# Two-layer state-space kernel, part A: turn tables relative to each 512-step chunk, kept in SBUF, and one wide multiply and one wide add for each turn

## The chip, the cores and the metric

The kernel runs on one core of one Trainium2 chip. The metric is the device time of one execution in microseconds (us), from the first to the last instruction. The core has five engines that work side by side, each through its own list of instructions, strictly in the order of that list: TensorE (PE, matrix products), VectorE (DVE), ScalarE (ACT), GpSimd (POOL) and SyncE (SP, which here only issues transfers). ACT and POOL issue transfers (DMAs) as well.

## The reference

The input is `x` (2048 steps of 640 channels) for part A, and `q`, `k`, `v` of the same shape for part B. The two results stand side by side in the output, 2048 x 1280, bfloat16. Part A is a diagonal complex recurrence over the steps; part B shifts and multiplies `k` and `v`, convolves along the steps by a 4096-point transform and multiplies with `q`.

```python
# part A
dt = exp(log_dt);  Lam_bar = exp(dt * Lam)               # 640 complex states
B_bar = ((Lam_bar - 1.0) / Lam)[:, None] * Bmat
Bu = einsum("bld,pd->blp", x, B_bar)
for t in range(L):  h = Lam_bar * h + Bu[:, t, :]
y = 2.0 * einsum("blp,dp->bld", hseq, Cmat).real + x * Dskip
# part B
kv = (k shifted by 0..3 steps, weighted with shift_k, summed) * v
y = irfft(rfft(kv_pad) * rfft(ssm_k_pad))[:S]
return concat([a, q * (y + kv * ssm_D)], axis=-1)
```

## The kernel before

**Part A.** The 2048 steps are cut into 4 chunks `c` of 512 steps, the 640 states into 5 blocks `j` of 128 (states on partitions, steps along the free axis). `block(c, j)` forms the real and imaginary input with ten matmuls (L352, L355), ACT casts them out of PSUM as `z` (L358, [128, 2, 512] bfloat16), and DVE does the rest. The complex recurrence is made real: the input is turned back by the angle of the state's own rotation at each step (`wre`, `wim`: four multiplies and two adds, L366 to L371), two scans with the real decay `rr` run along the 512 steps (L376, L377), and the result is turned forward again (`hre`, `him`: six instructions, L386 to L391). All of these are 128x512 instructions in bfloat16. The last element of each scan is copied (L381, L382) and starts the scan of the next chunk. After the fifth block of a chunk `project(c)` multiplies the ten `h` tiles with the output matrices: four groups of 20 matmuls (L406, L407) and a few for the skip term (L415), each group cast by ACT as `yo` (L418) and sent out by a transfer that POOL issues.

The angle counts from step 0 of the whole sequence. The sine and cosine of the first 512 steps (`tb_base`) are made once for each `j` by `build_tables` (a multiply on POOL, L316, which writes `tb_ph`; three passes on ACT, L318 to L321) and are written to a table in DRAM (`trig_tab`, L322, issued by POOL). Every block but the first fetches its table again (`tbase`, L337, issued by POOL). In the chunks c = 1, 2, 3 the table is turned by the chunk's start angle: two passes on ACT (`tbA`, `tbB`, L344, L345) and two scalar-tensor-tensor instructions on DVE (`sct`, L347, L348).

**Part B.** The channels are cut into 5 groups `G` of 128. `front(G)` transposes `k` and `v` in (L483, L484, issued by SP), makes `kvT` on DVE (L493, three L495, L497, 2048 wide), and stages it with eight transfers (`kv_st`, L500, SP) and the filter with eight more (`h_st`, L491, SP); a first transform stage on PE is cast by ACT as `As` (L454), a second as `Hf` (L514). `back1(G)` transforms `kv` (`Xs`, L535) and multiplies in frequency on DVE (`pw`, `Y`, 30 instructions). `back2(G)` transforms back on PE, casts four `Zs` (L581), transposes them as `Zt` by a transfer that ACT issues (L583), multiplies with the constant `Mq` (32 matmuls, L593, two halves of 16), and DVE multiplies each half with `q` out of PSUM (`ob`, two L595). POOL issues the transfer out.

Constants for part B are built at the start: `build_G` makes `Gre`, `Gim`, `nGim` in six rounds (an index pattern `t_v` at L102 and a multiply `t_ph` at L104 on POOL, four passes on ACT that end with `Gre`, L112). `build_Mq` makes `Mq`: a small multiply of `m_cv` (128x64, L161) and four multiplies (L164) on POOL, after a cosine on ACT.

**What sets the order.** The source emits blocks of part A at marked points of part B. A scheduler then fixes one list for every engine, from which no engine departs, and tiles that share a name or a tag share a buffer: who writes next waits for the last reader. So a change of a few instructions, or of a tile's tag, can move instructions of other parts of the kernel.

## Time and profile before

| | |
|---|---|
| median of 3 runs | 354.78 us (353.11, 354.78, 356.89) |
| span of the profiled execution | 354.2 us |
| DVE busy | 282.7 us (80%), 619 instructions |
| PE busy | 235.3 us (66%), 1896 matmuls |
| ACT busy | 173.1 us (49%) |
| POOL busy | 85.3 us (24%) |
| mean granted clock of PE | 0.877 of full speed |

The profile records one execution, not one of the three timed ones; the time of that execution is its span, and no other time for it is given. "DVE" and the other names stand for instructions of that engine; "SPq", "ACTq" and "POOLq" are the issuing of transfers by these engines, "issue" in the chain is time in which the engine waited for nothing that the profile shows. In a row of the timeline the first number is the start in us from the beginning of the span, the second the duration; what stands in brackets is the idle time of the engine just ahead of the row and what ended it. In the view of waits the three numbers are the idle time in all, the number of waits, and the longest.

### The profile page before, as it was taken

The page shows a single profiled execution, that of the slowest core. Times are in us where ns is not written, and L with a number is a line of the kernel's source. Part 1 is how long each engine was busy: PE and PEld are TensorE (multiplying, and loading weights), DVE is VectorE, ACT ScalarE, POOL GpSimd, SP SyncE. Part 2 cuts the span into 40 slices and gives each one's busy share as a digit, 9 for nine tenths or more (in the row PEclk, how much of TensorE's full clock was granted, in tenths as well). Part 3 has the DMA queues.
Part 4 walks back from the last instruction along what each step waited for, and adds up shares of the span by engine and source line. Part 5 has one row for each costly group of instructions (what it writes and reads, how often), then busy time and mean ns, then how long its engine had stood idle before and what let it go on. Part 6 is the DMA issues. An engine that isn't in the chain of part 4 may idle for free.

```text
span 354.2 us, 5098 instructions
## 1 busy us (share of the span) xinstructions
PE 235.3 (66%) x1896; PEld 150.7 (43%) x1896; DVE 282.7 (80%) x619; ACT 173.1 (49%) x231; POOL 85.3 (24%) x99
## 2 busy tenths in 40 slices
PE   0058179303799874757898198588499997675591
PEld 0013055301564542544655065265286554464371
DVE  3809999984999999998970799999974896989502
ACT  3548748303357484246564216478254795245020
POOL 2943639993120000020210001001041000020021
PEclk9998859856699999699999789589699999699698
DMA  5999997101035544283757704020664012232312
GB/s 95 197 209 213 205 213 150 44 0 61 19 102 141 112 105 108 71 161 64 179 137 153 170 1 121 20 71 30 148 166 149 1 31 54 66 102 61 76 57 78
DMA packets 89802, 36.68 MB, mean 104 GB/s; under 512 B 76465, under 2 KB 86706, under 8 KB 89778
## 3 DMA queue, kind: packets, MB, share of 16 engines
q1 hardware_dynamic: 65330, 18.01, 25.6%
q0 software_dynamic: 3808, 13.11, 12.5%
q10 hardware_dynamic: 20640, 5.24, 6.5%
q8 instruction: 15, 0.25, 0.3%
q14 instruction: 9, 0.07, 0.1%
HBM read 9.19 MB, written 6.55 MB: 44 GB/s over the span
## 4 chain that ended last, share of the span: by engine, by line
issue 36%; DVE 24%; POOL 12%; PE 9%; SPq 8%; DMA 6%; ACT 3%; ACTq 1%; POOLq 0%; DVEq 0%
POOL m_cv L161 7%; DVE kvT L495 4%; DVE uim L377 2%; PE psB L452 2%; DVE ure L376 2%; SPq L483 2%; DMA Zt<-Zs 2%; DMA out_dram<-yo 2%; PE psB L593 2%; SPq L500 1%; PE psA L406 1%; DMA vT<-in_B_v_dram 1%; PE psA L407 1%; SPq L209 1%; ACTq L583 1%
## 5 line engine op out<-in xcount | busy, mean ns | idle before, releaser
L406 PE MATMUL psA<-Csre,hre 128*128 128x320 bf16 x160 | 49.2, 330 | 40.8 <-DVE hre L388 21.0
L352 PE MATMUL psA<-xT,BTre 128*128 128x512 bf16 x100 | 31.1, 417 | 32.5 <-DMA xT<-in_A_x_dram 20.9
L407 PE MATMUL psA<-Csimn,him 128*128 128x320 bf16 x160 | 49.1, 327 | 1.3 <-DVE him L391 1.2
L337 POOL DMA_DIRECT2D tbase<-trig_tab x15 | 10.8, 721 | 120.4 <-DVE sct L348 75.5
L535 ACT CAST Xs<-psB 128x1024 bf16<-128x1024 f32 (+1 forms) x25 | 21.9, 886 | 36.1 <-PE psB L475 18.5
L358 ACT CAST z<-psA 128x1024 bf16<-128x1024 f32 x20 | 20.1, 1014 | 26.4 <-PE psA L355 15.5
L407 PEld LDWEIGHTS <-him 128*128 128x128 bf16 x160 | 16.7, 105 | 30.2 <-issue 18.7
L406 PEld LDWEIGHTS <-hre 128*128 128x128 bf16 x160 | 16.4, 105 | 30.2 <-DVE hre L388 24.4
L352 PEld LDWEIGHTS <-BTre 128*128 128x128 bf16 x100 | 10.1, 104 | 43.6 <-issue 25.6
L593 PE MATMUL psB<-Mq,Zt 128*128 128x256 bf16 x160 | 24.3, 323 | 6.6 <-DMA Zt<-Zs 6.6
L452 PE MATMUL psB<-R,h_st 128*128 128x512 bf16 x80 | 24.6, 449 | 5.9 <-ACT As_h L454 2.1
L514 ACT CAST Hf<-psB 128x1024 bf16<-128x1024 f32 (+1 forms) x25 | 21.0, 891 | 15.2 <-PE psB L475 10.6
L355 PE MATMUL psA<-xT,BTim 128*128 128x512 bf16 x100 | 27.7, 391 | 0.0
L161 POOL TENSOR_TENSOR m_cv<-m_cv,m_coef 128x64 f32<-128x64 f32 x1 | 25.2, 25237 | 4.1 <-ACT m_cv L50 4.1
L418 ACT CAST yo<-psA 128x640 bf16<-128x640 f32 x16 | 11.0, 694 | 28.6 <-PE psA L415 22.9
L454 ACT CAST As_h<-psB 128x1024 bf16<-128x1024 f32 x20 | 19.9, 1012 | 9.4 <-PE psB L452 9.4
L595 DVE TENSOR_TENSOR ob<-psB,qin 128x1024 bf16<-128x1024 f32 x10 | 12.1, 1217 | 15.0 <-PE psB L593 15.0
L593 PEld LDWEIGHTS <-Zt 128*128 128x128 bf16 x160 | 18.5, 117 | 12.8 <-DMA Zt<-Zs 7.5
L420 POOL DMA_DIRECT2D out_dram<-yo x16 | 8.9, 559 | 55.0 <-ACT yo L418 54.9
L344 ACT ACTIVATE tbA<-tbase,rot_s 128x512 bf16<-128x512 bf16 x15 | 10.9, 725 | 22.7 <-DVE sct L347 19.0
L598 POOL DMA_DIRECT2D out_dram<-ob x5 | 5.9, 1178 | 63.6 <-DVE ob L595 63.6
L581 ACT CAST Zs<-psB 128x1024 bf16<-128x1024 f32 x20 | 19.6, 1011 | 1.4 <-PE psB L580 1.4
(629 smaller groups left out, 780.9 us busy)
## 6 DMA issues: line engine op xcount, KB each, us to landing
tbase<-trig_tab POOLq DMA_DIRECT2D x15, 256.0 KB, 3.3
qin<-in_B_q_dram POOLq DMA_DIRECT2D x5, 512.0 KB, 6.3
h_st<-in_B_ssm_k_dram SPq DMA_DIRECT2D x40, 64.0 KB, 2.1
kv_st<-kvT SPq DMA_DIRECT2D x40, 64.0 KB, 2.4
out_dram<-yo POOLq DMA_DIRECT2D x16, 160.0 KB, 2.1
out_dram<-ob POOLq DMA_DIRECT2D x5, 512.0 KB, 4.6
trig_tab<-tb_base POOLq DMA_DIRECT2D x5, 256.0 KB, 5.0
kT<-in_B_k_dram SPq DMA_TRANSPOSE x5, 6.7
```

Of the source, the lines that this page charges most:

```text
L161: g.tensor_tensor(out=cv[:], in0=cv[:], in1=bq(coef), op=ALU.mult)
L352: nc.tensor.matmul(pz[:, 0, :], lhsT=self.BTre[:, k, j * 128:(j + 1) * 128], rhs=xT[:, k, :], start=(k == 0), stop=(k == NT - 1))
L355: nc.tensor.matmul(pz[:, 1, :], lhsT=self.BTim[:, k, j * 128:(j + 1) * 128], rhs=xT[:, k, :], start=(k == 0), stop=(k == NT - 1))
L358: nc.scalar.copy(out=z[:], in_=pz[:])
L406: nc.tensor.matmul(py[:, b, 0:320], lhsT=Hs[j][0][:, ts], rhs=self.Csre[:, j, c0:c0 + 320], start=(j == 0), stop=False)
L407: nc.tensor.matmul(py[:, b, 0:320], lhsT=Hs[j][1][:, ts], rhs=self.Csimn[:, j, c0:c0 + 320], start=False, stop=False)
L452: nc.tensor.matmul(pa[:, i, :], lhsT=st[:, d8, a_lo * 128:(a_lo + 1) * 128], rhs=self.C.R[:, a_lo, :], start=(a_lo == 0), stop=(a_lo == 1))
L454: nc.scalar.copy(out=As[:, :, 32 * pr:32 * pr + 32].rearrange("p k (i g) -> p k i g", i=2), in_=pa[:].rearrange("p i (g k) -> p k i g", k=32))
L514: nc.scalar.copy(out=Hf[:, :, pos * 128:(pos + n) * 128], in_=pt[:, :, 0:n * 128])
L535: nc.scalar.copy(out=Xs[:, :, 0:W], in_=pt[:, :, 0:W])
L581: nc.scalar.copy(out=Zs[:, qd, :, :].rearrange("p s (c k) -> p s c k", k=8), in_=pzf.rearrange("p (k s c) -> p s c k", k=8, s=8))
L593: nc.tensor.matmul(pyf[:, s4 * 256:(s4 + 1) * 256], lhsT=Zt[:, qd, st_, :], rhs=C.Mq[:, qd, :], start=(qd == 0), stop=(qd == 3))
```

## The change

Two things change in part A, and one line in the building of `Gre`.

The angle now counts from the start of each chunk. One table for each `j` then serves all four chunks, and it stays in SBUF: `tab` [128, 5, 3, 512], whose three slots hold -sin, cos and sin (the first is made by a new multiply by -1 on DVE, line 320 of the new kernel). Slots 0 and 1 and slots 1 and 2, read as two overlapping pairs, give one operand of shape [128, 2, 2, 512]. At the end of a chunk the state is turned by the angle of 512 steps: three instructions on two elements (`cm` twice, `cr`), in the place of the two copies. `trig_tab`, the fetches `tbase`, the ACT passes `tbA` and `tbB` and the two `sct` instructions are gone.

Each turn is now one multiply of 128x2048 (`pr`, line 345; `po`, line 363), whose other operand, `z` or the scan's result `u`, is repeated through a step of zero, and one add of 128x1024 (`w`, line 347; `h`, line 365), in the place of six 128x512 instructions. The scans are as they were.

In `build_G` the index pattern `t_v` now shares the buffer of `t_aph`, the intermediate of the cosine; the next round's pattern then waits for ACT's `Gre` of the round before. The temporaries `cs_tmp` share buffers of `w` and `u`.

```diff
-            v = tp.tile([128, 3, 128], i32, name="t_v")
+            v = tp.tile([128, 3, 128], i32, name="t_v", tag="t_aph")
...
-        self.hpool = ctx.enter_context(tc.tile_pool(name="a_h", bufs=2 * NT + 2))
-        self.dram = ctx.enter_context(tc.tile_pool(name="a_dram", bufs=1, space=bass.MemoryType.DRAM))
-        self.tab = self.dram.tile([NT, 2, 128, CW], bf16, name="trig_tab")
+        self.hpool = ctx.enter_context(tc.tile_pool(name="a_h", bufs=NT + 1))
...
-                tmp = ctp.tile([128, D], bf16, name="cs_tmp")
+                tmp = self.work.tile([128, D], bf16, name="cs_tmp", tag="w")
...
+        self.rot = self.small.tile([128, 2, NT, 2], f32, name="rot")
+        nc.scalar.activation(out=self.rot[:, 1, :, 0], in_=phc[:], func=ACT.Sin, scale=SC)
+        nc.scalar.activation(out=self.rot[:, 1, :, 1], in_=phc[:], func=ACT.Sin, scale=-SC)
...
+        self.tab = self.const.tile([128, NT, 3, CW], bf16, name="tab")
...
     def build_tables(self, j, tp):
-        nc = self.nc
+        nc = self.nc
+        tab = self.tab[:, j, :, :]
         ph = tp.tile([128, CW], i32, name="tb_ph", tag="t_ph")
         nc.gpsimd.tensor_tensor(out=ph[:], in0=self.lo_idx[:], in1=self.Fi[:, j:j + 1].to_broadcast([128, CW]), op=ALU.mult)
-        base = self.tbpool.tile([128, 2, CW], bf16, name="tb_base")
-        nc.scalar.activation(out=base[:, 0, :], in_=ph[:], func=ACT.Sin, scale=SC)
         aph = tp.tile([128, CW], f32, name="tb_aph", tag="t_aph")
         nc.scalar.activation(out=aph[:], in_=ph[:], func=ACT.Abs, scale=SC)
-        nc.scalar.activation(out=base[:, 1, :], in_=aph[:], func=ACT.Sin, bias=self.hpi[:, 0:1], scale=-1.0)
-        nc.gpsimd.dma_start(out=self.tab[j].rearrange("s p t -> p s t"), in_=base[:])
-        return base
+        nc.scalar.activation(out=tab[:, 2, :], in_=ph[:], func=ACT.Sin, scale=SC)
+        nc.scalar.activation(out=tab[:, 1, :], in_=aph[:], func=ACT.Sin, bias=self.hpi[:, 0:1], scale=-1.0)
+        nc.vector.tensor_scalar_mul(out=tab[:, 0, :], in0=tab[:, 2, :], scalar1=-1.0)
...
-            nc.gpsimd.dma_start(out=base[:], in_=self.tab[j].rearrange("s p t -> p s t"))
...
-            nc.scalar.activation(out=tA[:], in_=base[:, 1, :], func=ACT.Copy, scale=sb)
-            nc.scalar.activation(out=tB[:], in_=base[:, 1, :], func=ACT.Copy, scale=cb)
-            sct = work2.tile([128, 2, CW], bf16, name="sct")
-            nc.vector.scalar_tensor_tensor(out=sct[:, 0, :], in0=base[:, 0, :], scalar=cb, in1=tA[:], op0=ALU.mult, op1=ALU.add)
-            nc.vector.scalar_tensor_tensor(out=sct[:, 1, :], in0=base[:, 0, :], scalar=nsb, in1=tB[:], op0=ALU.mult, op1=ALU.add)
...
-        nc.vector.tensor_tensor(out=t1[:], in0=cosT, in1=zre, op=ALU.mult)
-        nc.vector.tensor_tensor(out=t2[:], in0=sinT, in1=zim, op=ALU.mult)
-        nc.vector.tensor_tensor(out=wre[:], in0=t1[:], in1=t2[:], op=ALU.add)
...
+        one = self.tab[:, j, 0, :]
+        tab = bass.AP(one.tensor, one.offset, [one.ap[0], [CW, 2], [CW, 2], [1, CW]])
+        sh = [128, 2, 2, CW]
+
+        pr = work2.tile(sh, bf16, name="pr", tag="pp")
+        nc.vector.tensor_tensor(out=pr[:], in0=tab, in1=z[:].rearrange("p (o b) t -> p o b t", o=1).to_broadcast(sh), op=ALU.mult)
+        w = work.tile([128, 2, CW], bf16, name="w")
+        nc.vector.tensor_tensor(out=w[:], in0=pr[:, :, 0, :], in1=pr[:, :, 1, :], op=ALU.add)
...
+            m = self.small.tile([128, 2, 2], f32, name=f"cm{j}_{c % 2}")
+            last = u[:, :, CW - 1]
+            nc.vector.tensor_tensor(out=m[:, 0, :], in0=last, in1=self.rot[:, 0, j, :], op=ALU.mult)
+            nc.vector.tensor_tensor(out=m[:, 1, :], in0=u[:, ::-1, CW - 1], in1=self.rot[:, 1, j, :], op=ALU.mult)
+            cr = self.small.tile([128, 2], f32, name=f"cr{j}_{c % 2}")
+            nc.vector.tensor_tensor(out=cr[:], in0=m[:, 0, :], in1=m[:, 1, :], op=ALU.add)
+            self.carry[j] = cr
+
+        po = work2.tile(sh, bf16, name="po", tag="pp")
+        nc.vector.tensor_tensor(out=po[:], in0=tab, in1=u[:].rearrange("p a (o t) -> p a o t", o=1).to_broadcast(sh), op=ALU.mult)
+        h = self.hpool.tile([128, 2, CW], bf16, name="h", tag="h")
+        nc.vector.tensor_tensor(out=h[:], in0=po[:, 0, :, :], in1=po[:, 1, :, :], op=ALU.add)
```

The change also moves instructions that it doesn't name, at three places on which the prediction rests.

On POOL, at the start of the program, the list before has the multiply of `m_cv` and the four of `Mq` behind three of the table multiplies `tb_ph` and their transfers:

```order
L316 TENSOR_TENSOR tb_ph<-tb_lo,Fi 128x512 x2
L322 DMA trig_tab<-tb_base 128x2x512
L316 TENSOR_TENSOR tb_ph<-tb_lo,Fi 128x512
L322 DMA trig_tab<-tb_base 128x2x512
L337 DMA tbase<-trig_tab 128x2x512
L161 TENSOR_TENSOR m_cv<-m_cv,m_coef 128x64
L164 TENSOR_TENSOR Mq<-m_cv,m_mask 128x256 x4
L316 TENSOR_TENSOR tb_ph<-tb_lo,Fi 128x512
L322 DMA trig_tab<-tb_base 128x2x512 x2
```

The list after has them inside the rounds of `build_G` (`t_v`, `t_ph`), and the four table multiplies come at the end:

```order
L104 TENSOR_TENSOR t_ph<-t_v,g_bsh 128x384
L161 TENSOR_TENSOR m_cv<-m_cv,m_coef 128x64
L164 TENSOR_TENSOR Mq<-m_cv,m_mask 128x256 x4
L102 IOTA t_v 128x384
L104 TENSOR_TENSOR t_ph<-t_v,g_bsh 128x384
L102 IOTA t_v 128x384
L104 TENSOR_TENSOR t_ph<-t_v,g_bsh 128x384
L102 IOTA t_v 128x384
L104 TENSOR_TENSOR t_ph<-t_v,g_bsh 128x384
L102 IOTA t_v 128x256
L104 TENSOR_TENSOR t_ph<-t_v,g_bsh 128x256
L315 TENSOR_TENSOR tb_ph<-tb_lo,Fi 128x512 x4
```

The five POOL instructions of `Mq` moved ahead by four rounds of `build_G` and three table multiplies; the cosine on ACT that `m_cv` waits for moved with them, to just behind its absolute value (L49). On PE the products with `Mq` are the L593 of `back2(0)`.

On SP, in the middle of the program, the transposes of `x` for chunk 3 (`xT`) and of `k` and `v` for group 4, and the staging of `kv` for group 3 (the first `kv_st`), stand like this before:

```order
L330 DMA_TRANSPOSE xT<-in_A_x_dram 128x5x512
L483 DMA_TRANSPOSE kT<-in_B_k_dram 128x2048
L500 DMA kv_st<-kvT 128x1x256 x8
L484 DMA_TRANSPOSE vT<-in_B_v_dram 128x2048
L491 DMA h_st<-in_B_ssm_k_dram 128x256 x8
L500 DMA kv_st<-kvT 128x1x256 x8
```

and like this after:

```order
L457 DMA_TRANSPOSE kT<-in_B_k_dram 128x2048
L458 DMA_TRANSPOSE vT<-in_B_v_dram 128x2048
L327 DMA_TRANSPOSE xT<-in_A_x_dram 128x5x512
L474 DMA kv_st<-kvT 128x1x256 x8
L465 DMA h_st<-in_B_ssm_k_dram 128x256 x8
L474 DMA kv_st<-kvT 128x1x256 x8
```

The staging of group 3's `kv` has moved behind one more transpose. The same shift of SP's transposes against the rest shows in `back2`: transposes are held one behind another, so `Zt` (issued by ACT) waits until SP's transposes that are ahead of it have landed. `Zt` of group 0 had only transposes up to `vT` of group 2 ahead of it; it now has the `kT` of group 3 ahead of it as well, whose buffer comes free only when DVE has made the `kvT` of group 2.

On DVE, at the end of chunk 2, the last block's `him` is followed before by the end of `kvT` for group 4 and by `sct` of the next chunk, and `ob` of group 2 stands between them:

```order
L391 TENSOR_TENSOR him<-t_2790,t_2791 128x512
L495 SCALAR_TENSOR_TENSOR kvT<-kT,sk_3018,kvT 128x2048
L347 SCALAR_TENSOR_TENSOR sct<-tbase,rot_c,tbA 128x512
L497 TENSOR_TENSOR kvT<-kvT,vT 128x2048
L348 SCALAR_TENSOR_TENSOR sct<-tbase,rot_ns,tbB 128x512
L347 SCALAR_TENSOR_TENSOR sct<-tbase,rot_c,tbA 128x512
L595 TENSOR_TENSOR ob<-psB,qin 128x16x64
```

and after, `ob` follows at once:

```order
L363 TENSOR_TENSOR po<-tab,u 128x2048
L359 TENSOR_TENSOR cr_0_2528<-cm_0_2525 128x2
L365 TENSOR_TENSOR h<-po 128x1024
L569 TENSOR_TENSOR ob<-psB,qin 128x16x64 x2
L513 TENSOR_TENSOR pw_2466<-Xs,Hf 128x512
```

What stood between the last block and `ob` has gone or has moved ahead. On PE, the L593 matmuls that this `ob` reads (L567 in the new kernel) stood behind 13 matmuls of `project(2)` that read the last block (L406, L407), and now stand behind 33.

On ACT, the cast `z` of block (3, 2), the third of the last chunk, stood ahead of the issue of `Zt` for group 3 (L583) and now stands behind it.

More of the change, by code (lines that the diff above doesn't have):

```diff
@@ L368, in block @@
-        nc.vector.tensor_tensor(out=wre[:], in0=t1[:], in1=t2[:], op=ALU.add)
-        nc.vector.tensor_tensor(out=t3[:], in0=cosT, in1=zim, op=ALU.mult)
-        nc.vector.tensor_tensor(out=t4[:], in0=sinT, in1=zre, op=ALU.mult)
-        nc.vector.tensor_tensor(out=wim[:], in0=t3[:], in1=t4[:], op=ALU.subtract)
-        ure = work.tile([128, CW], bf16, name="ure")
-        uim = work.tile([128, CW], bf16, name="uim")
-        ini_re, ini_im = (0.0, 0.0) if self.carry[j] is None else (self.carry[j][0][:, 0:1], self.carry[j][1][:, 0:1])
+        one = self.tab[:, j, 0, :]
@@ L375, in block @@
         rb = self.rr[:, j:j + 1].to_broadcast([128, CW])
-        nc.vector.tensor_tensor_scan(out=ure[:], data0=rb, data1=wre[:], initial=ini_re, op0=ALU.mult, op1=ALU.add)
-        nc.vector.tensor_tensor_scan(out=uim[:], data0=rb, data1=wim[:], initial=ini_im, op0=ALU.mult, op1=ALU.add)
+        for i in range(2):
+            ini = 0.0 if self.carry[j] is None else self.carry[j][:, i:i + 1]
+            nc.vector.tensor_tensor_scan(out=u[:, i, :], data0=rb, data1=w[:, i, :], initial=ini, op0=ALU.mult, op1=ALU.add)
@@ L378, in block @@
         if c < NCH - 1:
-            cre = self.small.tile([128, 1], f32, name=f"cre{j}_{c % 2}")
-            cim = self.small.tile([128, 1], f32, name=f"cim{j}_{c % 2}")
-            nc.vector.tensor_copy(out=cre[:], in_=ure[:, CW - 1:CW])
-            nc.vector.tensor_copy(out=cim[:], in_=uim[:, CW - 1:CW])
-            self.carry[j] = (cre, cim)
-        hre = self.hpool.tile([128, CW], bf16, name="hre", tag="h")
-        him = self.hpool.tile([128, CW], bf16, name="him", tag="h")
-        nc.vector.tensor_tensor(out=t1[:], in0=cosT, in1=ure[:], op=ALU.mult)
@@ L644 @@
         for j in range(1, NT):
-            bj = pa.build_tables(j, tpool)
-            pa.block(0, j, bj)
+            pa.build_tables(j, tpool)
+            pa.block(0, j)
         C.build_H()
```

56 lines of the change are left out of this document (14 added, 42 removed).

## The prediction

> **What bounds the kernel now.** I began with the totals and the chain of work that ended last, went on to DVE's waits, and then to DVE's own list inside one block. The page's head, the busy times and the chain's shares:
>
> ```profile
> span 354.2 us, 5098 instructions
> PE 235.3 (66%) x1896; PEld 150.7 (43%) x1896; DVE 282.7 (80%) x619; ACT 173.1 (49%) x231; POOL 85.3 (24%) x99
> issue 36%; DVE 24%; POOL 12%; PE 9%; SPq 8%; DMA 6%; ACT 3%; ACTq 1%; POOLq 0%; DVEq 0%
> ```
>
> DVE is the busiest engine, and it is idle for 354.2 - 282.7 = 71.5 us. The longest single waits of DVE:
>
> ```profile
> DVE ob L595 <- PE psB L593: 15.0, 5, 12.5
> DVE kvT L493 <- DMA kv_st<-kvT: 11.6, 1, 11.6
> DVE sk_360 L488 <- DMA sk_b_358<-in_B_shift_k_dram: 9.3, 1, 9.3
> DVE t_726 L366 <- ACT tb_base L321: 6.3, 1, 6.3
> ```
>
> So DVE sets the end nearly everywhere: less DVE work shortens the program one for one until something DVE waits for becomes late. Four holes (start, `t_726`, the one before `kvT` of group 4, the tail's 12.5) are not DVE's own work, and don't shrink because it is faster. All sums below are made against the profiled 354.2 us. The median of the timed runs, 354.78, lies 0.6 above it; I carry no correction for that.
>
> **The change part by part.** *One block, c = 1, 2, 3.* One whole block of chunk 2 on DVE, from its first `sct` to the next block's:
>
> ```profile
> 237.56 0.73 DVE L347 SCALAR_TENSOR_TENSOR sct<-tbase,rot_c,tbA 128x512 bf16<-128x512 bf16 x1
> ...
> 238.89 0.41 DVE L367 TENSOR_TENSOR t_2644<-sct,z 128x512 bf16<-128x512 bf16 x1
> 239.22 0.41 DVE L366 TENSOR_TENSOR t_2643<-sct,z 128x512 bf16<-128x512 bf16 x1
> ...
> 240.57 1.27 DVE L376 TENSOR_TENSOR_SCAN ure<-rr,cre_1_1572,wre 128x512 bf16<-128x512 f32 x1
> 241.76 0.39 DVE L371 TENSOR_TENSOR wim<-t_2645,t_2646 128x512 bf16<-128x512 bf16 x1
> ...
> 243.99 0.13 DVE L382 CAST cim_0_2660<-uim 128x1 f32<-128x1 bf16 x1
> 244.05 0.40 DVE L387 TENSOR_TENSOR t_2644<-sct,uim 128x512 bf16<-128x512 bf16 x1
> ...
> 245.39 0.73 DVE L347 SCALAR_TENSOR_TENSOR sct<-tbase,rot_c,tbA 128x512 bf16<-128x512 bf16 x1
> ```
>
> The block takes 245.39 - 237.56 = 7.83 us without a gap. Instructions overlap a little, so I count from start to start: 0.33 for a 128x512 multiply, 1.19 for a scan, 0.06 for a copy. The wide forms have near relatives: the 2048-wide multiply of `kvT`, and a 1920-wide add whose one operand repeats through a step of zero, as in the new multiplies:
>
> ```profile
> 256.14 1.21 DVE L497 TENSOR_TENSOR kvT<-kvT,vT 128x2048 bf16<-128x2048 bf16 x1
> 257.27 0.73 DVE L348 SCALAR_TENSOR_TENSOR sct<-tbase,rot_ns,tbB 128x512 bf16<-128x512 bf16 x1
> ...
> 279.07 1.14 DVE L507 TENSOR_TENSOR As_h<-As_h,drow 1x1920 bf16<-1x1920 bf16 x1
> ...
> 27.55 0.75 DVE L493 TENSOR_SCALAR kvT<-kT,sk_360 128x2048 bf16<-128x2048 bf16 x1
> 28.34 2.80 DVE L495 SCALAR_TENSOR_TENSOR kvT<-kT,sk_360,kvT 128x2048 bf16<-128x2048 bf16 x1
> ```
>
> Start to start the 2048-wide multiply takes 1.13 us, and the repeated operand costs no more per element (1.14/1920 against 1.21/2048). Between 0.33 at 512 and 1.13 at 2048, a 1024-wide add lies at 0.60. The last two rows are one instruction that reads what the one ahead wrote: 0.79 from start to start at 0.75 long, where independent ones overlap by 0.08, so such a pair loses some 0.1. The new block has about three (`pr`, `w`, scan; `po`, `h`). The sum: 2 x 1.13 + 2 x 0.60 + 2 x 1.19 + 3 x 0.06 + 0.3 = 6.32. Saved: 7.83 - 6.32 = 1.5 us a block, **22 us** over 15 blocks. Nearly all of it is the two `sct` (1.33); twelve narrow turns take 12 x 0.33 = 4.0, four wide ones 3.46, and the dependent pairs and the rotation of the carry (0.2) eat that.
>
> The Trainium skill (VectorE: DVE Perf Modes, the section on the TRN2 errata) says that every DVE instruction pays a fixed part of about 150 cycles once, so that one large instruction beats many small ones. By its formula the twelve narrow turns would cost 5.1 us and the four wide ones 3.8, 25 us less over 20 blocks where the rows give 11 (0.54 each): an estimate from that page by which the sum would be 329. The rows differ: narrow instructions start 0.33 us apart at 0.41 length, so about half of that fixed part is already hidden, and I go by them.
>
> *Chunk 0* has no `sct`:
>
> ```profile
> 64.84 0.41 DVE L366 TENSOR_TENSOR t_628<-tb_base,z 128x512 bf16<-128x512 bf16 x1
> ...
> 71.55 0.41 DVE L366 TENSOR_TENSOR t_677<-tb_base,z 128x512 bf16<-128x512 bf16 x1
> ```
>
> That is 6.71 a block, against 6.32 and about 0.25 for the new slot of `tab` (a 128x512 one-operand multiply, between a quarter of L493 and L366's spacing). I count nothing.
>
> *POOL's rows at the start.* DVE's third hole comes from POOL: `m_cv` held POOL for 25 us, and the table multiply for block 3 was queued behind it:
>
> ```profile
> 52.91 25.24 POOL L161 TENSOR_TENSOR m_cv<-m_cv,m_coef 128x64 f32<-128x64 f32 x1 [4.12 <-ACT m_cv L50]
> ...
> 39.43 3.12 POOL L316 TENSOR_TENSOR tb_ph<-tb_lo,Fi 128x512 int32<-128x512 int32 x1 [1.32 <-ACT tb_aph L320]
> ...
> 27.34 0.17 DVE L488 CAST sk_360<-sk_b_358 128x4 f32<-128x4 bf16 x1 [9.31 <-DMA sk_b_358<-in_B_shift_k_dram]
> 37.15 1.24 DVE L387 TENSOR_TENSOR t_326<-tb_base,uim 128x512 bf16<-128x512 bf16 x1
> ```
>
> `m_cv` began at 52.91 and ended at 78.15, when DVE had run dry. It is a small instruction, so it was starved, not slow. In the new order it stands among the rounds of `build_G`, at some 21 to 24 us, while DVE idles until 27.34. There it should run at once, and the hole goes: **+6.3**. The other direction is also in the rows: a DVE instruction that meets a POOL one is stretched (1.24 at 37.15, where 0.41 is usual). POOL's rounds are now gated by ACT and reach further into DVE's work; two more such meetings cost **-1.5** (0 to -3).
>
> The Trainium skill (SBUF — State Buffer, Who interferes with whom) says that VectorE and GpSimd share a port under an exclusive lock, held for a whole instruction, and that the second one waits for the first to finish. That speaks against long DVE instructions, yet by it a POOL multiply would wait at most one of them, 1.2 us. The 25 us of `m_cv` don't fit that: here POOL got in only when DVE stopped.
>
> *SP's order.* DVE's 11.6 us hole:
>
> ```profile
> 182.34 1.22 DVE L497 TENSOR_TENSOR kvT<-kvT,vT 128x2048 bf16<-128x2048 bf16 x1
> ...
> 181.42 3.34 SPq L330 DMA_TRANSPOSE xT<-in_A_x_dram  x1
> ...
> 187.37 5.52 SPq L500 DMA_DIRECT2D kv_st<-kvT  x8
> 192.93 2.15 SPq L484 DMA_TRANSPOSE vT<-in_B_v_dram  x1
> 195.20 0.75 DVE L493 TENSOR_SCALAR kvT<-kT,sk_3018 128x2048 bf16<-128x2048 bf16 x1 [11.62 <-DMA kv_st<-kvT]
> ```
>
> `kvT` of group 4 may overwrite the buffer only when `kv_st` of group 3 has landed, 195.20 - 192.89 = 2.3 us after its last issue. Before, from the end of L497 (183.56) to 195.20 it is 11.6. After, `vT` (whose buffer that same L497 frees) and `xT` come first: 2.15 + 3.34 + 5.52 + 2.3 = 13.3. **-1.5** (0 to -2.5); this hole stays.
>
> *`Zt` of group 0* now waits for the `kT` of group 3, which waits for DVE's last L495 of group 2:
>
> ```profile
> 137.93 4.14 ACTq L583 DMA_TRANSPOSE Zt<-Zs  x1
> ...
> 152.82 4.89 SPq L483 DMA_TRANSPOSE kT<-in_B_k_dram  x1
> ```
>
> From that L495 the way to `ob` is `kT` 4.9, `Zt` 4.1, half of the 32 matmuls 2.0 to 2.7, and two landings of some 1 to 2 us each: 13 to 15. DVE has two scans, the L497, a `po`, and the next block up to its `po` to do meanwhile, 11 us. **-3** (0 to -5).
>
> *`ob` of group 2* now stands right behind the last block of chunk 2. PE before:
>
> ```profile
> 253.01 0.45 PE L406 MATMUL psA<-Csre,hre 128*128 128x320 bf16 x1 [5.32 <-DVE hre L388]
> ...
> 255.98 4.00 PE L593 MATMUL psB<-Mq,Zt 128*128 128x256 bf16 x32
> ```
>
> Sixteen matmuls (13 that read the last block, three L415) took 2.97 us at PE's clock after an idle stretch. Now 33 and six stand there: 39/16 x 2.97 = 7.2 us, or 4.5 at the full clock, and then half of the 4.00. DVE's wait is 6.5 to 9.2; before it had 5.4 us of work in that place and didn't wait. **-8**.
>
> *`z` of block (3, 2)* now follows the issue of `Zt` of group 3 on ACT:
>
> ```profile
> 298.16 4.06 ACTq L583 DMA_TRANSPOSE Zt<-Zs  x1
> ...
> 299.07 0.43 DVE L366 TENSOR_TENSOR t_3457<-sct,z 128x512 bf16<-128x512 bf16 x1 [3.46 <-ACT z L358]
> ```
>
> DVE already waits 3.46 us for that cast; 4.06 more would come ahead of it, less what ACT is earlier. **-3** (0 to -4). ACT's and POOL's own savings (`tbA`, `tbB`, `tbase`) count nothing: neither is DVE's releaser in a long wait but for those named.
>
> The sum: 22 + 6.3 - 1.5 - 1.5 - 3 - 8 - 3 = 11.3; 354.2 - 11.3 = 342.9, say **343 us**. With each term at its better end it is 332, at its worse end 353.
>
> **The rivals.** *No new waits.* If `Zt`, `kv_st`, `z` and PE's list turn out on time, 22 + 6.3 - 1.5 remains, 327 us. For it: some of these engines are earlier too. Against: the queues' lists are fixed, and PE cannot go round the 33 matmuls.
>
> *Widening pays its fixed part as well.* If the narrow spacing of 0.33 hides a stall that wide instructions don't have, about 0.09 us for each of eight instructions saved in 20 blocks, 14 us more: 329. The Trainium skill's page VectorE: DVE Perf Modes, cited above, would have it so. Against it is the 1.13 of the 2048-wide row, which leaves no room.
>
> *The gain is given back.* DVE waits at the next transfer or matmul for what it saved: only `m_cv`'s hole goes and the new waits come, 351 to 356. For it: 27 of DVE's idle microseconds hang on PE and on `kv_st`. Against: between those waits DVE runs blocks back to back, with `z` ready.
>
> *`m_cv` starves again, earlier* (slower). It must start before DVE wakes at 27.34. If the gated rounds of POOL bring it later, it can be held like before, now with four rounds of `build_G` and all tables behind it: DVE would run out of work after `kvT` and block (0, 0), about 17 us on, and then wait for them. That costs the 6.3 and some 16 us more: 359 to 366. The margin, 3 us, is against it.
>
> *The wide multiply runs at half speed* (slower). The slow form shows here:
>
> ```profile
> 258.60 1.21 DVE L595 TENSOR_TENSOR ob<-psB,qin 128x1024 bf16<-128x1024 f32 x1
> ```
>
> 1.21 us for 1024 elements, twice L497's price. Should the overlapping slots bring that about, `pr` and `po` cost 1.1 more each, 45 us over 20 blocks: 388. From 1.9 us on the new block is as long as the old. L507, with its step of zero, is against it; slots that overlap stand in no row.
>
> **How the numbers follow.** Under 1% (3.5 us) a run of this kernel tells no change: faster means below 351.2, slower above 358.3. The chances: the forecast 0.57 (0.04 of it within 1%), no new waits 0.15, the fixed part too 0.03, gain given back 0.14 (0.01 of it faster), `m_cv` 0.06 (0.02 within 1%), half speed 0.05. Faster: 0.53 + 0.15 + 0.03 + 0.01 = 0.72; the same: 0.04 + 0.13 + 0.02 = 0.19; slower: 0.04 + 0.05 = 0.09. The range takes in the forecast's bounds, the case where the gain is given back, and the nearer half of the full gain: 327 to 356.
>
> **What would show it.** In the profile after: a block of about 6.3 us with `pr` at 1.2 and `w` at 0.7; `m_cv` under 2 us and no wait for `tab` after block 2 of chunk 0; a wait of 6 to 9 us at the third `ob`, 2 to 5 at the first; some 13 us before `kvT` of group 4; `z` as the releaser of `pr` near the end. It is wrong if `pr` takes over 1.5 us, if `m_cv` is long, or if the waits named are not there.

## The result, and the profile after

The new kernel took 342.7 us (median of four runs, 339.4 to 344.9), against 355.8 for the kernel before on the same chips. The ratio is 0.961, with a 95% interval of 0.951 to 0.972. The forecast was 343, with a range of 327 to 356. The profiled execution, with a span of 343.1 us and a time of 344.9, is the slowest of the four and lies 1.6% above the fastest; the ratios, and the medians of the experiments, leave out executions more than 1.5% above the fastest of their kernel, and so counted the new kernel's median is 341.9. In all four runs the time lies 1.7 to 1.8 above the span. The forecast was a sum of differences against one profiled span (354.2), so it is compared with spans: 11.3 us less was forecast, 11.1 came. (Between the medians it is 13.1.)

The page's head after:

```profile
span 343.1 us, 4834 instructions
...
PE 233.6 (68%) x1896; PEld 152.2 (44%) x1896; DVE 256.1 (75%) x449; ACT 155.0 (45%) x202; POOL 47.9 (14%) x79
...
DVE 40%; PE 19%; SPq 12%; issue 9%; DMA 9%; ACT 5%; POOL 3%; ACTq 1%; POOLq 0%; DVEq 0%
```

DVE's busy time fell by 282.7 - 256.1 = 26.6 us, but the span by 11.1 only: DVE's idle time rose from 71.5 to 87.0, by 15.5. The same view of DVE's waits as before shows where it idles now:

```profile
DVE ob L569 <- PE psB L567: 25.6, 5, 11.4
DVE kvT L467 <- DMA kv_st<-kvT: 21.6, 2, 20.0
DVE sk_341 L462 <- DMA sk_b_339<-in_B_shift_k_dram: 9.1, 1, 9.1
DVE pr L345 <- ACT z L338: 7.8, 2, 7.5
DVE pw_2673 L513 <- ACT Xs L509: 3.7, 1, 3.7
```

`ob` went from 15.0 to 25.6, `kvT` from 11.6 to 21.6, the cast `z` from 5.3 (3.5 and 1.8) to 7.8. The 6.3 us for the table of block 3 are gone. One whole block of chunk 2 in DVE's timeline (start and duration in us, engine, line, operation, tiles, shapes), from one `pr` to the next; the `h` in it is that of the block ahead:

```profile
231.38 1.22 DVE L345 TENSOR_TENSOR pr<-tab,z 128x2048 bf16<-128x2048 bf16 x1
232.51 0.69 DVE L365 TENSOR_TENSOR h<-po 128x1024 bf16<-128x1024 bf16 x1
233.11 0.69 DVE L347 TENSOR_TENSOR w<-pr 128x1024 bf16<-128x1024 bf16 x1
233.83 2.46 DVE L352 TENSOR_TENSOR_SCAN u<-rr,cr_1_1422,w 128x512 bf16<-128x512 f32 x2
236.33 0.16 DVE L356 TENSOR_TENSOR cm_0_2401<-u,rot 128x2 f32<-128x2 bf16 x1
...
236.48 1.22 DVE L363 TENSOR_TENSOR po<-tab,u 128x2048 bf16<-128x2048 bf16 x1
...
237.68 1.22 DVE L345 TENSOR_TENSOR pr<-tab,z 128x2048 bf16<-128x2048 bf16 x1
```

From `pr` to `pr` it takes 6.30 us, where 6.32 was forecast and 7.83 stood before. The repeated operand and the overlapping slots cost nothing that these rows show: 1.22 us for 2048 elements, against L497's 1.21 in the kernel before. And `m_cv` in POOL's timeline:

```profile
19.22 0.29 POOL L161 TENSOR_TENSOR m_cv<-m_cv,m_coef 128x64 f32<-128x64 f32 x1
```

0.29 us in the place of 25.24: the instruction is not slow in itself, as the forecast said.

### The profile page after: what moved, and what is told of

The parts are those of the page before. It is cut to its first block, busy times and chain, and to the rows that moved or that the text cites. A ratio compares the mean times of both kernels' runs of the same rounds, so it can differ in the third digit from the quotient of the medians.

```text
span 343.1 us, 4834 instructions
## 1 busy us (share of the span) xinstructions
PE 233.6 (68%) x1896; PEld 152.2 (44%) x1896; DVE 256.1 (75%) x449; ACT 155.0 (45%) x202; POOL 47.9 (14%) x79
## 4 chain that ended last, share of the span: by engine, by line
DVE 40%; PE 19%; SPq 12%; issue 9%; DMA 9%; ACT 5%; POOL 3%; ACTq 1%; POOLq 0%; DVEq 0%
DVE u L352 9%; DVE kvT L469 5%; DVE pr L345 5%; DVE po L363 4%; PE psA L380 4%; PE psA L381 4%; PE psB L426 3%; SPq L474 3%; DVE w L347 3%; DMA kv_st<-kvT 3%; DMA Zt<-Zs 3%; PE psB L567 2%; DVE h L365 2%; SPq L327 2%; DMA out_dram<-yo 2%
## 5 line engine op out<-in xcount | busy, mean ns | idle before, releaser
L380 PE MATMUL psA<-Csre,h 128*128 128x320 bf16 x160 | 50.2, 330 | 39.9 <-DVE h L365 34.8
L381 PE MATMUL psA<-Csimn,h 128*128 128x320 bf16 x160 | 50.0, 330 | 0.0
L332 PE MATMUL psA<-xT,BTre 128*128 128x512 bf16 x100 | 29.2, 401 | 30.4 <-DMA xT<-in_A_x_dram 20.3
L380 PEld LDWEIGHTS <-h 128*128 128x128 bf16 x160 | 17.0, 106 | 44.8 <-DVE h L365 38.8
L569 DVE TENSOR_TENSOR ob<-psB,qin 128x1024 bf16<-128x1024 f32 x10 | 12.2, 1218 | 25.6 <-PE psB L567 25.6
L345 DVE TENSOR_TENSOR pr<-tab,z 128x2048 bf16<-128x2048 bf16 x20 | 25.0, 1251 | 7.8 <-ACT z L338 7.8
L392 ACT CAST yo<-psA 128x640 bf16<-128x640 f32 x16 | 11.1, 692 | 41.2 <-PE psA L389 40.8
L488 ACT CAST Hf<-psB 128x1024 bf16<-128x1024 f32 (+1 forms) x25 | 21.1, 890 | 11.1 <-PE psB L449 11.1
L567 PE MATMUL psB<-Mq,Zt 128*128 128x256 bf16 x160 | 24.7, 327 | 1.1 <-DMA Zt<-Zs 1.1
L426 PE MATMUL psB<-R,h_st 128*128 128x512 bf16 x80 | 21.1, 402 | 6.4 <-ACT As_h L428 2.7
L363 DVE TENSOR_TENSOR po<-tab,u 128x2048 bf16<-128x2048 bf16 x20 | 24.4, 1220 | 0.1
L567 PEld LDWEIGHTS <-Zt 128*128 128x128 bf16 x160 | 18.6, 118 | 7.8 <-DMA Zt<-Zs 2.5
L381 PEld LDWEIGHTS <-h 128*128 128x128 bf16 x160 | 16.8, 105 | 11.4 <-issue 5.8
L447 PEld LDWEIGHTS <-nGim 128*128 128x128 bf16 x150 | 15.7, 105 | 12.3 <-issue 12.1
```

What stands on the lines that cost most here:

```text
L332: nc.tensor.matmul(pz[:, 0, :], lhsT=self.BTre[:, k, j * 128:(j + 1) * 128], rhs=xT[:, k, :], start=(k == 0), stop=(k == NT - 1))
L345: nc.vector.tensor_tensor(out=pr[:], in0=tab, in1=z[:].rearrange("p (o b) t -> p o b t", o=1).to_broadcast(sh), op=ALU.mult)
L363: nc.vector.tensor_tensor(out=po[:], in0=tab, in1=u[:].rearrange("p a (o t) -> p a o t", o=1).to_broadcast(sh), op=ALU.mult)
L380: nc.tensor.matmul(py[:, b, 0:320], lhsT=Hs[j][0][:, ts], rhs=self.Csre[:, j, c0:c0 + 320], start=(j == 0), stop=False)
L381: nc.tensor.matmul(py[:, b, 0:320], lhsT=Hs[j][1][:, ts], rhs=self.Csimn[:, j, c0:c0 + 320], start=False, stop=False)
L426: nc.tensor.matmul(pa[:, i, :], lhsT=st[:, d8, a_lo * 128:(a_lo + 1) * 128], rhs=self.C.R[:, a_lo, :], start=(a_lo == 0), stop=(a_lo == 1))
```

## The experiments

Twelve kernels were run. Each is compared with runs of the kernel before on the same chip; since that kernel's median there was 357 to 359, the ratios are the better measure, with spans of the profiled executions beside them. "The new kernel" below is the one of the change, ratio 0.961, span 343.1.

### One part alone: the buffer that t_v shares

```diff
# in the kernel before
-            v = tp.tile([128, 3, 128], i32, name="t_v")
+            v = tp.tile([128, 3, 128], i32, name="t_v", tag="t_aph")
```

> The kernel before with one edit of the change alone: the index pattern t_v of build_G shares the buffer of t_aph. POOL's multiply of m_cv then stands behind the third round of build_G and no longer behind the table multiplies. Theory (m_cv was starved because it fell into DVE's busy stretch): it takes under 1 us if it comes before DVE wakes at 25 to 27 us, DVE's wait of 6.3 us for the table of block 3 goes, and the span falls by 4 to 6 us, to 348 to 350. Rival (starved wherever it stands after DVE has woken, here perhaps at 22 to 28 us): m_cv long again, with rounds of build_G behind it, 355 to 370. Second rival (the 6.3 us come back at a later wait): 353 to 355.

The ratio is 0.990 (0.981 to 0.998), the span 350.4. POOL's timeline has:

```profile
23.81 0.29 POOL L161 TENSOR_TENSOR m_cv<-m_cv,m_coef 128x64 f32<-128x64 f32 x1
```

The wait for the table is gone, and of its 6.3 us 3.8 reach the end by the two spans, 1.0% by the ratio. So about a quarter to a third of the whole gain comes from a tag in the constants of part B, not from the turn tables; the interval, 0.2 to 1.9%, leaves it open how much exactly. It does not tell why `m_cv` starved: it shows only that the same instruction runs at once where DVE is idle.

### Widening undone

```diff
# in the new kernel; the same for po and h
-        nc.vector.tensor_tensor(out=pr[:], in0=tab, in1=z[:]...to_broadcast(sh), op=ALU.mult)
-        nc.vector.tensor_tensor(out=w[:], in0=pr[:, :, 0, :], in1=pr[:, :, 1, :], op=ALU.add)
+        for a in (1, 0):
+            for b in (0, 1):
+                nc.vector.tensor_tensor(out=pr[:, a, b, :], in0=self.tab[:, j, a + b, :], in1=z[:, b, :], op=ALU.mult)
+        for a in (1, 0):
+            nc.vector.tensor_tensor(out=w[:, a, :], in0=pr[:, a, 0, :], in1=pr[:, a, 1, :], op=ALU.add)
```

> The new kernel with its resident relative tables and its rotation of the carry, but each turn as four 128x512 multiplies and two 128x512 adds again, on the same tiles. Theory (the rows: narrow instructions start 0.33 us apart, so twelve cost 4.0 us a block where the four wide ones take 3.6): DVE's time in turns goes up by 0.4 to 0.5 us a block, 8 to 10 us in all, and the span by 5 to 10 us less what the order gives or takes, 345 to 353 against the new kernel's 343. Rival (every instruction pays its fixed part, as the page on VectorE's modes has it, 1.26 us a block): DVE's time in turns goes up by 25 us, the span to 360 or more. Second rival (DVE's gain is given back in waits anyway): no change, 341 to 345.

The ratio is 0.959 (0.948 to 0.971), the span 340.2: no slower than with wide turns. In the DVE timeline of the narrow kernel a block takes 6.59, from the first row to the second:

```profile
230.41 1.41 DVE L348 TENSOR_TENSOR pr<-tab,z 128x512 bf16<-128x512 bf16 x4
...
237.00 1.41 DVE L348 TENSOR_TENSOR pr<-tab,z 128x512 bf16<-128x512 bf16 x4
```

Counting every instruction from its start to the next one's start, turns take 81.5 us of DVE here, 71.9 in the new kernel and 81.7 before: 0.48 us a block, near the 0.54 of the rows. The fixed part in the Trainium skill (VectorE: DVE Perf Modes, the section on the TRN2 errata) would make it 1.25, an estimate by that page's formula; the trace doesn't agree. The block shown gains 0.29; in the wide form the scans and the small instructions behind them, which wait for the one ahead, take a little longer. DVE is busy for 265.1 us here, against 256.1.

That none of it shows at the end doesn't mean that it is worth nothing there, because the scheduler set the order anew, and one difference of order matters. Here `Zt` of group 0 (ACT's queue) goes out before `kT` of group 3 (SP's queue):

```profile
126.40 4.80 ACTq L563 DMA_TRANSPOSE Zt<-Zs  x1
...
141.11 2.60 SPq L463 DMA_TRANSPOSE kT<-in_B_k_dram  x1
```

In the new kernel it is the other way round:

```profile
127.45 2.05 SPq L457 DMA_TRANSPOSE kT<-in_B_k_dram  x1
...
132.05 6.18 ACTq L557 DMA_TRANSPOSE Zt<-Zs  x1
```

So DVE waits nowhere at the first `ob` here, where it waits 5.8 us in the new kernel. The next experiment gives the wide kernel that same order and has a span of 335.8; against it the narrow turns lose 4.4 us. This run is therefore no test of widening alone.

### The first ob: Zt of group 0 and kT of group 3

```diff
+        if G == 3:   # kT of group 3 behind Zt of group 0: an edge of order, without a semaphore of its own
+            self.tc.add_manual_dep(kt.ins, PartB.zt0.ins.name, ...)
```

> The new kernel, with the transpose kT of group 3 held behind Zt of group 0, in the place of the other way round; the list of every engine is the same as in the new kernel. Theory of the prediction (Zt waits for that kT, and ob of group 0 for Zt): DVE's wait of 5.8 us at the first ob falls to under 1.5, the span by up to 4, 339 to 341. Rival (kv_st of group 2, behind kT on SP, now comes late and the gain is given back at kvT of group 3 or 4): the first wait falls, the span stays at 342 to 345.

The ratio is 0.941 (0.934 to 0.947), the span 335.8: the largest single gain. The lists of all engines are those of the new kernel; only which of the two transposes waits for the other has changed. `Zt` starts at 124.30 where it had started at 132.05. DVE's timeline at the first `ob` in the new kernel, and then here (in brackets the wait ahead of the instruction and what ended it):

```profile
144.25 1.23 DVE L569 TENSOR_TENSOR ob<-psB,qin 128x1024 bf16<-128x1024 f32 x1 [5.76 <-PE psB L567]
```

```profile
139.71 1.23 DVE L573 TENSOR_TENSOR ob<-psB,qin 128x1024 bf16<-128x1024 f32 x1 [1.05 <-PE psB L571]
```

The forecast's step was right in kind. The wait fell by 4.7 and the span by 7.3: the wait before `kvT` of group 4 is shorter too, 17.2 in the place of 20.0, because `kv_st` lands 3.3 us after its last issue here and 6.0 in the new kernel (why is taken up below). So the rival (given back there) falls.

### The cast z behind the issue of Zt of group 3

```diff
-        nc.scalar.dma_start_transpose(out=Zt[:]...
+        (nc.sync if G == 3 else nc.scalar).dma_start_transpose(out=Zt[:]...
```

> The new kernel, with the transpose Zt of group 3 issued by SP, whose list is empty by then, in the place of ACT, so that the casts z behind it needn't wait for its issue. Theory of the prediction (z of block (3, 2) is late because it stands behind 4 to 5 us of issue): DVE's wait of 7.5 us near 285 falls to 2 to 4, the span by 3 to 5 us, 338 to 340. Rival (z waits for its matmuls on PE or for Zs, not for the issue): the wait stays at 6 or more. Second rival (ob of group 3 takes the gain): the wait falls, the span doesn't.

The ratio is 0.951 (0.942 to 0.959), the span 338.9. DVE's timeline with the wait in the new kernel, and then here:

```profile
292.39 1.23 DVE L345 TENSOR_TENSOR pr<-tab,z 128x2048 bf16<-128x2048 bf16 x1 [7.50 <-ACT z L338]
```

```profile
286.17 1.23 DVE L345 TENSOR_TENSOR pr<-tab,z 128x2048 bf16<-128x2048 bf16 x1 [2.60 <-ACT z L338]
...
329.46 1.23 DVE L569 TENSOR_TENSOR ob<-psB,qin 128x1024 bf16<-128x1024 f32 x1 [13.70 <-PE psB L567]
```

4.9 us of wait went, as forecast, and 2.3 came back at the last `ob`, whose wait was 11.4. The medians (340.7 against 341.9) have ranges that overlap, so how much reaches the end is not shown; the trace shows the wait itself.

### The third ob: PE's list

```diff
+                    if c == 2 and j == NT - 1:   # matmuls of project(2) on the last block, behind those of ob of group 2
+                        self.tc.add_manual_dep(m.ins, PartA.ob_mm.ins.name, ...)
```

> The new kernel, with the matmuls of project(2) that read the last block held behind the matmuls for ob of group 2 on PE; the lists of DVE and SP are the same as in the new kernel. Theory of the prediction (the 33 matmuls ahead of it make that ob late): DVE's wait of 7.4 us there falls to under 2, the span by 5 to 6, 337 to 338. Rival (Zt of group 2 lands at about 248.5, only 1.6 us before PE reaches its matmuls, so PE's list matters little): the wait falls to 5.5 to 6, the span by 1 to 2, 341 to 342.

The ratio is 0.974 (0.963 to 0.986), the span 345.0: not faster. PE now stands idle where its 33 matmuls had been, and DVE waits as long as in the new kernel (7.2 against 7.4). PE's timeline of this run, and then DVE's:

```profile
247.88 5.09 PE L569 MATMUL psB<-Mq,Zt 128*128 128x256 bf16 x32 [7.38 <-DMA Zt<-Zs]
```

```profile
251.26 1.23 DVE L571 TENSOR_TENSOR ob<-psB,qin 128x1024 bf16<-128x1024 f32 x1 [7.20 <-PE psB L569]
```

`Zt` was issued at 241.17 and landed 6.7 us later. So the 33 matmuls filled a gap in which PE would have waited for `Zt`. In the new kernel `Zt` landed at 248.5, 1.6 us before PE was through with them. Even these 1.6 us, the rival's gain, didn't come, and PE's granted clock says why. These are two stretches of `--windows` on PE (from and to, length, PE's busy time and matmuls, granted clock, DMA's share and GB/s), first in this run and then in the new kernel:

```profile
248.00:250.00 2.00, 2.00 (x11) 0.50 0.00 0
```

```profile
250.00:252.00 2.00, 2.00 (x21) 1.00 0.13 44
```

Behind its idle 7.4 us PE runs at a granted clock of 0.50, and the first half of the matmuls takes 251.26 - 247.88 = 3.4 us; behind the 33 matmuls it runs at 1.00, and the same half takes 252.09 - 250.14 = 1.95. Moving the 33 behind makes them late elsewhere besides (the wait for `Xs` behind them grew from 3.7 to 7.4).

### The wait before kvT of group 4: SP's order

```diff
+        if G == 4:   # vT of group 4, and likewise xT of chunk 3, behind the last kv_st of group 3 on SP
+            self.tc.add_manual_dep(vt.ins, PartB.last_st.ins.name, ...)
```

> The new kernel, with the staging of kv for group 3 (kv_st) ahead of the transposes of v for group 4 and of x for chunk 3 on SP; nothing else moves on any engine. Theory (the 20 us wait before kvT of group 4 is SP's order, 7 us, and a collision with Zt of group 1, 6 us): kv_st is issued from 173.5, lands by 182, the wait falls to 8 to 10 us; the next wait is for the cast z behind the issue of Zt of group 1, so that of the 10 to 12 us some 5 to 8 reach the end: 335 to 338. Rival (the hole belongs to z and Zt, kvT is only the name on it): the wait moves to pr, the span stays within 1 us of 343. Second rival (all of it reaches the end): 331 to 333.

The ratio is 0.973 (0.963 to 0.984), the span 345.3. In the new kernel SP issued `kv_st` at 179.96, behind two transposes; here, ahead of both. SP's queue in the new kernel, and then here, with DVE's row under it:

```profile
171.16 2.20 SPq L457 DMA_TRANSPOSE kT<-in_B_k_dram  x1
173.46 2.98 SPq L458 DMA_TRANSPOSE vT<-in_B_v_dram  x1
176.53 3.34 SPq L327 DMA_TRANSPOSE xT<-in_A_x_dram  x1
179.96 6.44 SPq L474 DMA_DIRECT2D kv_st<-kvT  x8
```

```profile
180.87 6.30 SPq L478 DMA_DIRECT2D kv_st<-kvT  x8
187.21 2.07 SPq L460 DMA_TRANSPOSE vT<-in_B_v_dram  x1
...
189.69 0.75 DVE L471 TENSOR_SCALAR kvT<-kT,sk 128x2048 bf16<-128x2048 bf16 x1 [16.84 <-DMA kv_st<-kvT]
```

It starts no earlier. The transposes ahead of it had cost next to nothing, because `kv_st` waits for something else. What did change is its landing: 189.69 - 187.17 = 2.5 us after the last issue, where it was 192.38 - 186.40 = 6.0 in the new kernel. There `Zt` of group 1 ran at the same time (issued from 184.75 to 191.11); here `Zt` starts at 191.8, and then the casts behind it are late. In the runs of the two helpful edits above, `Zt` began only 0.6 us before the last issue ended, and `kv_st` landed 3.3 us after it. So some 3.5 us of the wait go with `Zt` at its side, a collision of transfers, and the theory of SP's order falls.

A second buffer for `kv_st` was to test what it waits for. It needs 4 KB, which one buffer less for `pr` and `po` gives:

```diff
-        pr = work2.tile(sh, bf16, name="pr", tag="pp")
+        pr = work.tile(sh, bf16, name="pr", tag="pp")
...
# the second run only
-        kv_st = self.stp.tile([128, 8, 256], bf16, name="kv_st")
+        kv_st = self.kvs.tile([128, 8, 256], bf16, name="kv_st")    # a pool of two buffers
```

> The new kernel, with one buffer in the place of two for the products pr and po, which frees 4 KB per partition for the run beside this one; DVE both writes and reads them, so no wait comes of it. It is the control for that run. On SP its kv_st for group 3 stands ahead of vT and xT, as in the run with the changed SP order. Every theory: 341 to 347, with a wait of 15 to 20 us ahead of kvT of group 4.

> The control with a second buffer for kv_st, so that the staging of group 3 needn't wait until PE has read group 2's; the lists of DVE, ACT, POOL and PE are those of the control. Theory (the 20 us wait is the chain from the last h of chunk 1 over project(1) on PE to the transform that reads kv_st of group 2, and SP's order never mattered): kv_st is issued right after kvT of group 3, near 174, and the wait falls to 8 to 11 us; the cast z behind Zt of group 1 comes next, so 3 to 6 us reach the end against the control. Rival (the transfers' own time holds it: kv_st is late even with a free buffer): no change of the wait. Second rival (z behind Zt takes all of it): the wait falls, the span stays within 1 us.

The ratios are 0.959 and 0.958, the spans 341.6 and 341.3. The pair says little: in both the scheduler had put DVE's work in another order, and the long wait is two waits of 7.5 to 8.3 us on `kv_st`. The second buffer changes neither. It could not: in that order `kv_st` of group 3 goes out 3.0 us after PE's last read of the buffer even with one, and 4.4 with two, so the buffer isn't what it waits for there.

The test that tells was on PE. In the list of the new kernel the matmuls that read `kv_st` of group 2, and so free its only buffer (16 of them; the expectation below says 32), stand behind `project(1)`, which needs the last `h` of chunk 1. In the run with the edit for `Zt` of group 0 one sees it: PE's last eight end at 175.88, and SP issues `kv_st` at 175.91, though the transpose ahead of it was through at 175.33.

```profile
173.94 1.94 PE L426 MATMUL psB<-R,kv_st 128*128 128x512 bf16 x8
...
175.91 5.92 SPq L476 DMA_DIRECT2D kv_st<-kvT  x8
```

This run puts the 16 ahead, on top of that edit:

```diff
-        self.yield_cb("f2")
+        if G != 2:
+            self.yield_cb("f2")
         As_kv = self._stage1(kv_st, "As_kv")
+        if G == 2:
+            self.yield_cb("f2")
```

> The kernel with kT of group 3 held behind Zt of group 0, and besides the block that front of group 2 emits put behind its transform of kv, so that on PE the 32 matmuls that read kv_st of group 2 stand ahead of project(1). Theory (the long wait before kvT of group 4 is the chain from the last h of chunk 1 over project(1) and these 32 matmuls to the buffer of kv_st): kv_st of group 3 is issued by 175, the wait falls from 17 to 10 or less, and 2 to 5 us reach the end: 330 to 334. Rival (the wait is set by Zt of group 1 and the casts behind it, whatever kv_st does): DVE waits as long in all, at kvT or at pr, 335 to 337.

The ratio is 0.925 (0.920 to 0.931), the span 330.0, 5.8 below the run without the swap (335.8). The wait in DVE's timeline without the swap, and then with it, SP's `kv_st` above:

```profile
185.11 0.75 DVE L469 TENSOR_SCALAR kvT<-kT,sk 128x2048 bf16<-128x2048 bf16 x1 [17.24 <-DMA kv_st<-kvT]
```

```profile
166.83 5.17 SPq L476 DMA_DIRECT2D kv_st<-kvT  x8
...
174.88 0.75 DVE L469 TENSOR_SCALAR kvT<-kT,sk 128x2048 bf16<-128x2048 bf16 x1 [8.75 <-DMA kv_st<-kvT]
...
187.28 1.23 DVE L345 TENSOR_TENSOR pr<-tab,z 128x2048 bf16<-128x2048 bf16 x1 [3.23 <-ACT z L338]
```

The wait is a chain over PE: last `h` of chunk 1, `project(1)`, the transform of group 2's `kv`, its buffer, `kv_st`, `kvT`. With the chain cut, `kv_st` goes out right behind the `kvT` that it stages, and of the 8.5 us of wait that go, 3.2 come back at the next cast.

### Together, and widening once more

> The two edits that helped, together: kT of group 3 held behind Zt of group 0, and Zt of group 3 issued by SP. Theory (the two waits lie in different stretches and add up): DVE's wait at the first ob about 1, at z of block (3, 2) 2 to 3, at the last ob 13 to 14; the span falls by 6 to 7 for the first and by 2 to 4 for the second, to 332 to 335, against 335.8 with the first alone. Rival (the second is eaten at the tail): 335 to 337.

With `kT` behind `Zt` of group 0 and `Zt` of group 3 on SP: ratio 0.934 (0.928 to 0.940), median 334.6. The waits are as expected (0.9 at the first `ob`, 2.6 at `z`, 13.6 at the last `ob`). The second edit adds little that the medians can tell.

> The run beside this one with narrow turns (four 128x512 multiplies and two adds for each turn). Theory (widening takes 10 us off DVE, which the waits at the first ob and elsewhere swallowed in the new kernel; with these waits gone it pays): narrow turns cost 4 to 10 us, 337 to 343. Rival (the other waits, before kvT of group 4, at the third ob and at z, swallow it still): 332 to 335, the same as wide turns.

The same with narrow turns: ratio 0.954 (0.948 to 0.960), median 342.0; only its times are used. The two intervals don't touch. Here narrow turns cost about 2%, some 7 us, in the forecast 4 to 10. The orders of PE and ACT differ a little between these two as well. The first narrow run (341.4) and this one (342.0) take about the same time, as they should if the first had the order of `Zt` and `kT` by itself. So widening pays when that order is the same on both sides, by 4.4 us (spans, the edit for `Zt` of group 0 alone) and 7 us (medians, this pair).

> All three edits together, with wide turns: kT of group 3 behind Zt of group 0, Zt of group 3 issued by SP, and the 32 matmuls of kv of group 2 ahead of project(1). Theory (the three waits add up): 328 to 332. Rival (only the first two count): 332 to 335.

All three edits: ratio 0.920 (0.913 to 0.927), median 330.3, span 329.1. This beats both kernels, the one before by 8% and the new one by some 4%. Its longest waits on DVE:

```profile
DVE ob L576 <- PE psB L574: 25.1, 7, 13.9
DVE kvT L469 <- DMA kv_st<-kvT: 10.5, 2, 8.8
DVE sk L464 <- DMA sk_b<-in_B_shift_k_dram: 10.1, 2, 8.6
DVE pr L345 <- ACT z L338: 7.2, 3, 4.1
```

## Why the prediction was right, point by point

The number came out by luck: two errors of some 16 us cancelled. DVE's work shrank by 6 more than forecast and small waits by 10, and the new waits were longer by about as much. The gains and the waits that it named were all there, but one of the waits had another cause. The account of DVE, in us of the span:

| term | forecast | measured |
|---|---|---|
| DVE's busy time, with POOL's holds | -20.5 | -26.6 |
| `m_cv`'s hole | -6.3 | -6.3 |
| a new wait at `sk` of group 1 | 0 | +2.3 (not in the run with the tag alone; cause open) |
| wait before `kvT` of group 4 | +1.5 | +8.4 |
| first `ob` | +3 | +5.8 |
| third `ob` | +8 | +7.9 |
| `z` of block (3, 2) | +3 | +4.0 |
| other new waits (`kvT` of group 2, dependent pairs) | in the block | +3.0 |
| waits that shrank (`Xs`, `As_h`, `z` of chunk 2, two `ob`), net of small new ones | 0 | -9.6 |
| sum | -11.3 | -11.1 |

*The block*: right, 6.30 against 6.32. The busy time fell by more because chunk 0 gained as well, which was counted at nothing: its twelve turns shrink by the same 0.5 us a block, and the new slot of `tab` costs 0.2. *`m_cv`*: right in kind and size at its place; run alone, 3.8 of the 6.3 us reach the end (by one span against one). *POOL's holds*: forecast 1.5 more; the stretched DVE instructions after 20 us add up to 4.8 us, against 4.0 before.

*SP's order*, the step "`vT` and `xT` come first", failed: the price was a sixth of what came, and the cause was another. I took the row in which `kv_st` stood behind two transposes for its reason, and didn't follow its buffer to PE. The chain from the last `h` of chunk 1 over PE to `kv_st` is as long as before (15.9 us against 15.8), so what DVE saves behind that `h`, 3.7 us, turns into waiting; the late landing beside `Zt` adds 3.7, and a longer issue of `kv_st` 0.9. In the kernel before, the queue did hold `kv_st` for the last 2.1 us of that chain; in the new kernel for 0.6 at most. *`ob` of group 2*, the step "PE cannot go round the 33 matmuls", described the path that the trace shows (5.4 us from the first of these matmuls to the last, then 1.95), but little hung on it: without the 33, `Zt` would have kept DVE waiting all but 1.6 of the 7.4 us, and with the lower clock it did for 7.2. That the size came out at 7.9 is luck in part. *`Zt` of group 0* and *`z`*: right in kind, mis-sized; the first measured 5.8 where 3 was taken, because `Zt` landed 9.1 us after its issue began, where it had taken 5.9. Most of that goes with `kv_st` beside it; but every `Zt` of the new kernel is slower, also alone: 6.7 us to landing, against 5.5 to 5.9 before and 5.5 to 5.6 in the run with the tag alone. So the change to part A makes `Zt` slower by about 1 us; the forecast took the old duration over, and the cause stays open.

*The unforecast gain*: some 10 us of smaller waits for casts of `Xs`, `As_h` and `z` shrank. They were counted as fixed. ACT is 18 us less busy (173.1 to 155.0) without `tbA` and `tbB`, which I had priced at nothing; that this is why those waits shrank was not tested.

The rivals: "widening pays its fixed part" is out by DVE's own time in the narrow run, 0.48 us a block where that rival has over 1.2. "No new waits" shows what was there for the taking: with the three edits 330 us, close to its 327, though not by the same waits. "The gain is given back" was half true: 15.5 of 26.6 us. One sum of the prediction is off: its bounds, each term at the worse end, add up to 350 and not 353; nothing else rests on it.

## What to carry to other kernels

When the busiest engine gets faster, price each of its long waits by the chain that ends it, from buffer to last reader, and not by the row that stands ahead of the late one in a queue: a queue's neighbour can be hidden under a longer wait. A chain that starts at this engine's own result and runs over others doesn't get shorter with it; the wait at its end grows by what the engine saves meanwhile (here 3.7 us). An edge of order between two transfers can be worth as much (7.3 us of 343 here) as a quarter of the busy engine's instructions. And when a part of a change is undone to price it, compare the order of the transfers first: here the scheduler had quietly removed a wait in the run without the part.

## What the runs showed of the hardware

The transfers that ran side by side here stretched each other. In the new kernel `Zt` takes 4.7 to 4.8 us to issue alone and 6.2 to 6.4 beside `kv_st` (in the kernel before 4.0 to 4.1, never beside `kv_st`). `kv_st` of group 3 lands 2.3 us after its last issue in the kernel before and 2.5 in the run with SP's order changed, both without `Zt`, and 6.0 beside `Zt`. The second case, in ACT's queue and DVE's timeline:

```profile
184.75 6.36 ACTq L557 DMA_TRANSPOSE Zt<-Zs  x1
...
192.38 0.76 DVE L467 TENSOR_SCALAR kvT<-kT,sk_2736 128x2048 bf16<-128x2048 bf16 x1 [19.98 <-DMA kv_st<-kvT]
```

A GpSimd multiply of 128x64 takes 0.29 us beside an idle VectorE and took 25.24 beside a busy one, while other GpSimd multiplies, met by the same kinds of VectorE instructions, were held for 2.5 us at most (a `tb_ph` took 3.50 in the run with the tag alone, and 1.04 at the start of that program). Here is another in POOL's timeline of the new kernel, which took 0.92 in the kernel before:

```profile
41.31 2.77 POOL L104 TENSOR_TENSOR t_ph<-t_v,g_bsh 128x256 int32<-128x256 int32 x1
```

The lock for one whole instruction that the Trainium skill (SBUF — State Buffer, Who interferes with whom) describes fits a `tb_ph` of 3.12 us in the kernel before, which met a VectorE instruction of 2.34. It fits neither `m_cv` nor this row, held for 1.8 us or more where the longest VectorE instruction beside it took 1.14; what makes the difference stays open. That wide instructions with an operand of overlapping slots or a step of zero run at the plain price, 1.22 us for 2048 elements in bfloat16, is shown by `pr` and `po`. And PE's granted clock was 0.50 behind an idle stretch of 7.4 us and 1.00 in the new kernel at the same matmuls, 3.4 us against 1.95 for sixteen of them.
